# Attention output of five batches with tokens on rows, turned by the DMA crossbar, in a fused attention and expert kernel

## The chip, the cores and the metric

The kernel runs on one core of one Trainium2 chip. A core has a matrix engine (PE), a vector engine (DVE), a scalar engine (ACT), a general engine (POOL) that also issues the loads here, and a queue engine (SP) that issues DMAs. The metric is device time of one execution in microseconds. The kernel before was timed three times: 159.49, 161.36 and 158.82 us, median 159.49. Beside this stands one profiled execution with its trace.

## What is computed

Eight batches of 576 tokens. The first stage is an attention of 8 heads of 64 dimensions, in which keys and values are averaged over 8 tokens, so that each head has 72 pooled keys:

```python
k_p = k.reshape(B, H, Sp, pool, D).mean(axis=3)          # v_p likewise
scores = scale * np.matmul(q, k_p.transpose(0, 1, 3, 2))
attn = np.exp(scores - max); attn /= attn.sum(-1) + 1e-09
attn_out = np.matmul(attn, v_p)                          # [8, 8, 576, 64]
x = attn_out.transpose(0, 2, 1, 3).reshape(B, S, 512)
```

The second stage takes x. A gate `x @ w_gate` has four logits a token, of which the two largest are kept and made into weights. Each of four experts is a causal attention of one head of 64 dimensions over the 576 tokens, with its own projections; its output goes through `wo[e]`, is multiplied by the gate's weight of that token and added up into out [8, 576, 512] float32.

## The kernel before, in words

All orders are written out by hand: a long string `SEQ` (line 591) of tokens `name:batch@bank`, which a loop translates into instructions. PE, ACT, DVE and POOL each run their instructions in the order in which they come in this string; a `d` behind a token puts a copy on DVE instead of ACT. SP's queue runs its DMAs in the same order. PSUM has eight banks, and a token says which one its product fills.

The 576 tokens of a batch are cut into four tiles of 128 and a tail of 64; two batches make a pair, whose tails share one tile. For each batch the tokens are, in order of dependence:

- `L_k`, `L_q`, `L_v`: loads, issued by POOL (line 118), ten DMAs a batch, into three rotating buffers of each kind (`NRAW`). They turn float32 into bf16 on the way. POOL also runs the causal masks `a` (lines 471 and 479) between them.
- `PK`, `kc`, `kt`: PE pools the keys by a product with a small matrix, DVE turns them, a copy makes them bf16. `PV`, `vc`: the same for values. `u`: DVE turns q (line 255).
- `E`, `e`: scores of all heads, with the 96 padded pooled keys on partitions and tokens along columns; ACT takes the exponential into `eta` (line 292).
- `D`, `d`, `x`: PE adds the exponentials up by a product with ones (`onesd`), in which every sum stands on 32 partitions; ACT takes its logarithm (line 311) and the exponential of minus that (line 315), which is one over the sum, into `rza`.
- `O`, `o`: PE multiplies the pooled values with `eta`, 32 value dimensions of a head a strip; DVE multiplies the product with `rza` and writes bf16 into `xT` (lines 329 and 338), which has the 512 features on partitions and tokens along columns. This is the form that the second stage needs.
- `V`, `v`: expert values and gate logits of a tile of tokens. `g`: ten steps of the gate. `P`, `p`: queries and keys of experts, in pairs. `S`, `s`: expert scores and their exponential (line 462) into `etb`. `B`, `bz`, `bg`, `b`: product with the values and a column of ones, one over the sum, times the gate (lines 514, 516, 521), into `osc`, with tokens on rows.
- Then `osc` is turned into `oT`. For batches 0, 1, 6 and 7 by PE (`T`, line 198) and a copy (`t`); for batches 2 to 5 by the DMA crossbar (`F`, function `crossbar`, lines 546 and 549), issued on SP.
- `Y`, `y`: the product with `wo` and its copy to `ofin`, which SP writes out (lines 580 and 584).

For batch 0 the first stage works on halves of 256 tokens. Copies share line 180 and products share line 189, so they are told apart by their tiles.

Of the kernel before, what the change touches and what calls it, by code (L numbers as in the profile page):

```python
# [21 lines left out]
def kernel(  # L22
# [26 lines left out]
    PAIRW = 128 * NPC  # L49
# [41 lines left out]
    oscs = bufs(4, [128, NTC, 128], BF16, "osc")  # L91
    oTs = bufs(4, [128, PAIRW], BF16, "oT")
# [114 lines left out]
    def mcols(b):  # L207
        return slice(640 * (b % 2), 640 * (b % 2) + MAIN)

    def tcols(b):  # L210
        return slice(MAIN + 64 * (b % 2), MAIN + 64 * (b % 2) + TAIL)

# [31 lines left out]
    def vc(b, bank, dve):  # L244
        copy(dve, vps[b % 2][:], psum[0:KR, bank, :].rearrange("j (h d) -> j h d", d=D))
# [72 lines left out]
    def Ov(b, bank, g, t):  # L318
        got = pieces(b, g)
        for j, cols, o in got:  # L320
            for u in range(2) if g == 2 else [t]:
                for i, h, eta in heads(b, j, cols):
                    at_ = o * 2 + TAIL * u if g == 2 else o
                    mm(psum[32 * i : 32 * i + 32, bank, at_ : at_ + eta.shape[1]], vps[b % 2][:, h, u::2], eta)

    def ov(b, bank, dve, g, t):
        xT, rz = xt(b), part(rzas[b % 2], b, g)
        if g == 2:
            nc.vector.tensor_tensor(
                out=xT[:, :, tcols(b)].rearrange("p (g t) n -> p g t n", t=2),  # L330
# [4 lines left out]
        else:  # L335
            got = pieces(b, g)
            m = mcols(b).start
            nc.vector.tensor_tensor(  # L338
                out=xT[:, 2 * got[0][0] + t : 2 * got[-1][0] + t + 1 : 2, m + got[0][1].start : m + got[0][1].stop],
                in0=psum[:, bank, :].rearrange("p (g n) -> p g n", g=len(got)), in1=rz, op=MULT,  # L340
            )

    def V(b, bank, c):
        for fc in range(NFC):
            wide(psum[:, bank, 0:VG], xt(b)[:, fc, 128 * place(b, c) : 128 * place(b, c) + 128], wvg[:, fc, :],
# [65 lines left out]
    def pcols(b, nm, h):  # L411
        if nm == "t":
            return tcols(b), MAIN, TAIL
        m, c, n = mcols(b).start, (0 if h is None else HALF * h), (MAIN if h is None else HALF)
        return slice(m + c, m + c + n), c, n

    def P(b, bank, nm, ep, h=None):
        jobs = [(m, e) for m in "qk" for e in range(NEP)] if nm == "t" else [(nm, ep)]
        cols, _, n = pcols(b, nm, h)
        for j, (m, e) in enumerate(jobs):  # L420
            for fc in range(NFC):
                wide(psum[:, bank, n * j : n * j + n], wqk[m, e][:, fc, :], xt(b)[:, fc, cols],
                   start=(fc == 0), stop=(fc == NFC - 1))

    def p(b, bank, dve, nm, ep, h=None):
        qk = qks[b % 2]
        _, c, n = pcols(b, nm, h)
# [57 lines left out]
    def span(b, part):  # L485
        if 2 <= b < B - 2:
# [244 lines left out]
```

## Time and profile before

| | |
|---|---|
| median of three runs | 159.49 us (158.82 to 161.36) |
| the profiled execution, its own time | 159.26 us |
| its span, first to last instruction | 157.6 us |
| PE, ACT, DVE, POOL busy | 91%, 85%, 79%, 57% of the span |
| loads issued by POOL | 15.21 MB in 60240 packets |
| `oT<-osc` crossbar DMAs on SP | 16 |
| PE's mean granted clock | 0.969 |

In the profile, a line of a group of instructions has the source line, the engine, the operation, the tile written and those read, the shape, the count, then the busy time in us, the mean duration of one in ns, and the idle time of the engine just ahead of them with what ended it. Products on PE overlap, so that the busy time of a group is that of their union. The line of a queue has packets, MB, and the time of the packets as a share of the 16 DMA engines' time; it can exceed 100% since a DMA engine has more than one packet under way. "DMA to landing" is the time from the issue to the completion. A window shows busy us of PE, PEld (the weight loads), DVE, ACT and POOL, each with the number of instructions, then the granted clock, the DMA engines' share, and GB/s.

### The profile page before, as it was taken

What the parts mean: (1) busy time and instruction counts of PE and PEld (TensorE: products, weight loads), DVE (VectorE), ACT (ScalarE), POOL (GpSimd) and SP (SyncE); (2) the same over time, 40 slices, a digit from 0 to 9 for tenths busy, and PEclk for the clock granted to TensorE, in tenths of its full rate; (3) what the DMA queues carried; (4) which work ended last, traced back from release to release, by engine and by line L of the source; (5) the groups of instructions that cost most, each with busy time, mean ns of one, the idle gap of its engine ahead of it and who ended that gap; (6) DMA issues with size and microseconds to landing.
All of it is one profiled execution on the core that took longest, in us unless ns stands there. A gap on an engine that the chain in (4) does not pass through costs nothing.

```text
span 157.6 us, 5500 instructions
## 1 busy us (share of the span) xinstructions
PE 143.9 (91%) x2155; PEld 82.8 (53%) x2155; DVE 124.4 (79%) x412; ACT 133.7 (85%) x249; POOL 90.5 (57%) x162
## 2 busy tenths in 40 slices
PE   6876798988999999999999899999999999999940
PEld 2333565545456356446545564857576665557620
DVE  1513567697999989998999889999998998898840
ACT  3016778999899999999999899999999999899740
POOL 6997479976989799897986342004500343533000
PEclk9998579999999999999999999999999999999996
DMA  2999999999999999999999994512213064487994
GB/s 19 161 173 180 181 179 179 188 179 182 180 182 180 180 180 181 178 249 181 180 245 249 179 148 108 37 50 60 80 28 104 8 177 131 124 320 264 344 354 146
DMA packets 70635, 26.20 MB, mean 166 GB/s; under 512 B 65744, under 2 KB 66000, under 8 KB 70608
## 3 DMA queue, kind: packets, MB, share of 16 engines
q0 software_dynamic: 60240, 15.21, 99.7%
q1 hardware_dynamic: 10144, 10.23, 21.2%
q10 hardware_dynamic: 224, 0.39, 0.9%
q8 instruction: 17, 0.28, 0.7%
q14 instruction: 10, 0.08, 0.2%
HBM read 30.42 MB, written 9.44 MB: 253 GB/s over the span
## 4 chain that ended last, share of the span: by engine, by line
PE 53%; DMA 23%; POOL 14%; issue 3%; DVE 2%; POOLq 0%; DVEq 0%
PE psum L189 52%; DMA kraw<-in_k_dram 18%; DMA qraw<-in_q_dram 5%; POOL kraw L118 4%; POOL vraw L118 3%; POOL qraw L118 3%; POOL etb L479 2%; PE psum L198 1%; POOL wst_q L131 1%; POOL wst_k L131 1%; DVE qT L255 1%; POOL wop L131 0%; DVE osc L521 0%; DVE ofin L180 0%; DVE G L406 0%
## 5 line engine op out<-in xcount | busy, mean ns | idle before, releaser
L462 ACT ACTIVATE etb<-psum 128x1024 bf16<-128x1024 f32 x48 | 47.6, 1033 | 1.1 <-PE psum L189 1.0
L479 POOL TENSOR_SCALAR_AFFINE_SELECT etb<-etb 128x256 bf16<-128x256 bf16 x64 | 25.5, 412 | 37.9 <-ACT etb L462 36.7
L292 ACT ACTIVATE eta<-psum 96x1024 bf16<-96x1024 f32 (+1 forms) x48 | 36.1, 812 | 4.7 <-PE psum L189 4.2
L118 POOL DMA_DIRECT2D qraw<-in_q_dram x32 | 21.2, 669 | 4.8 <-DMA vraw<-in_v_dram 2.2
L189 PEld LDWEIGHTS <-etb 128*128 128x128 bf16 x480 | 18.7, 97 | 7.2 <-issue 2.8
L338 DVE TENSOR_TENSOR xT<-psum,rza 128x512 bf16<-128x512 f32 x32 | 20.8, 684 | 1.7 <-ACT rza L315 1.4
L118 POOL DMA_DIRECT2D vraw<-in_v_dram x24 | 18.6, 777 | 6.2 <-DMA kraw<-in_k_dram 3.6
L189 PE MATMUL psum<-vaug,etb 128*128 128x65 bf16 x480 | 20.6, 193 | 0.1
L189 PE MATMUL psum<-xT,wqp 128*128 128x64 bf16 (+2 forms) x136 | 20.2, 282 | 0.1
L189 PE MATMUL psum<-wvg,xT 128*128 128x260 bf16 x144 | 20.0, 274 | 0.1
L189 PE MATMUL psum<-wop,oT 128*128 128x512 bf16 (+1 forms) x74 | 19.8, 374 | 0.2 <-DVE oT L180 0.2
L189 PE MATMUL psum<-xT,wkp 128*128 128x64 bf16 (+2 forms) x136 | 19.8, 279 | 0.0
L118 POOL DMA_DIRECT2D kraw<-in_k_dram x24 | 18.6, 785 | 1.7 <-POOLq L715 0.8
L521 DVE TENSOR_TENSOR osc<-psum,gt 128x256 bf16<-128x256 f32 (+2 forms) x40 | 16.5, 421 | 1.0
L189 PEld LDWEIGHTS <-xT 128*128 128x128 bf16 x144 | 12.7, 97 | 7.2 <-issue 3.7
L189 PE MATMUL psum<-qk 64*128 64x64 bf16 (+4 forms) x192 | 15.6, 277 | 0.2 <-ACT etb L462 0.2
L189 PE MATMUL psum<-eta,vp 96*32 96x64 bf16 (+2 forms) x272 | 14.1, 301 | 1.1 <-DVE vp L180 0.8
L189 PE MATMUL psum<-qT,kpT 32*128 32x64 bf16 (+2 forms) x272 | 12.7, 281 | 2.6 <-DVE qT L255 2.3
L255 DVE STREAM_TRANSPOSE qT<-qraw 128x576 f32<-128x576 f32 (+2 forms) x18 | 11.9, 690 | 3.7 <-DMA qraw<-in_q_dram 3.5
L180 ACT COPY ofin<-psum 128x512 f32<-128x512 f32 (+1 forms) x22 | 12.6, 591 | 1.6 <-PE psum L189 1.5
L180 DVE CAST qk<-psum 128x512 bf16<-128x512 f32 (+1 forms) x22 | 13.3, 611 | 0.7 <-PE psum L189 0.6
L315 ACT ACTIVATE rza<-rza 128x512 f32<-128x512 f32 (+1 forms) x24 | 12.5, 529 | 0.3
(75 smaller groups left out, 216.5 us busy)
## 6 DMA issues: line engine op xcount, KB each, us to landing
out_dram<-ofin SPq DMA_DIRECT2D x31, 256.0 KB, 3.5
kraw<-in_k_dram POOLq DMA_DIRECT2D x24, 192.0 KB, 7.8
qraw<-in_q_dram POOLq DMA_DIRECT2D x32, 144.0 KB, 7.6
vraw<-in_v_dram POOLq DMA_DIRECT2D x24, 192.0 KB, 7.2
out_dram<-ofin SPq DMA_DIRECT2D x7, 128.0 KB, 2.6
wst_q<-in_moe_wq_dram POOLq DMA_DIRECT2D x1, 256.0 KB, 7.4
wst_k<-in_moe_wk_dram POOLq DMA_DIRECT2D x1, 256.0 KB, 8.0
wst_v<-in_moe_wv_dram POOLq DMA_DIRECT2D x1, 256.0 KB, 8.3
```

Of the source, the lines that this page charges most:

```text
L118: nc.gpsimd.dma_start(out=dst, in_=src)
L131: nc.gpsimd.dma_start(out=dst, in_=src)
L180: (nc.vector.tensor_copy if dve else nc.scalar.copy)(out=out, in_=in_)
L189: nc.tensor.matmul(out=out, lhsT=lhsT, rhs=rhs, start=start, stop=stop)
L198: nc.tensor.transpose(out=out[s], in_=in_[:, s], identity=ident[0:n, 0:n])
L255: nc.vector.transpose(out=dst.rearrange("p (a s n) -> p a n s", s=32, n=2), in_=src.rearrange("p (a n d) -> p a n d", n=2, d=32))
L292: nc.scalar.activation(out=dst, in_=src, func=EXP, scale=ATT_EXP_SCALE)
L315: nc.scalar.activation(out=rz, in_=rz, func=EXP, scale=-1.0)
L338: nc.vector.tensor_tensor(out=xT[:, 2 * got[0][0] + t : 2 * got[-1][0] + t + 1 : 2, m + got[0][1].start : m + got[0][1].stop], in0=psum[:, ...
L462: nc.scalar.activation(out=et[:, ep, :, eo : eo + n], in_=psum[:, bank : bank + 2, 0:n], func=EXP, scale=MOE_EXP_SCALE,)
L479: nc.gpsimd.affine_select(out=blk, in_=blk, pattern=[[0, 2], [1, 128]], compare_op=ISGE, fill=0.0, base=0, channel_multiplier=-1,)
L521: nc.vector.tensor_tensor(out=osc(b, ep)[:, own, :].rearrange("p c (e d) -> p e c d", e=2), in0=o[:, :, :, 0:HD], in1=gt.to_broadcast([128 ...
```

## The change

Batches 3 to 7 no longer use `D`, `d`, `x`, `O` and `o`. A column is added to the pooled values of each head, with ones scaled as the values are. `N` (five a batch) multiplies, for each of the 8 heads, 128 tokens of `eta` as the stationary operand with the 65 columns of that head; the result has tokens on rows, and the last column of a head is its sum. `nz` inverts the 8 sums of a tile on DVE, and `n` multiplies the 8 x 64 outputs with them into `xn` in bf16, tokens on rows. `G` (three a batch: two of 128 x 1024, one of 64 x 512) has the DMA crossbar turn `xn` into `xT`, issued on SP. `rza`, which batches 0 to 2 still use, lies in the memory of `xn`.

`xT` is laid out tile by tile (`[128, NPC, NFC, 128]`), in another order of the features, which `rows_of` gives to those who read it; `vc` writes the values in a permuted order to match. The ones of the batch's tail need a pad behind `eta`. At the other end, `oT` and `osc` are laid out anew, and the crossbar turns the outputs of batches 0 to 5 (`F`, `turn_y`, three a batch: two of 128 x 512, one of 64 x 256), and PE those of batches 6 and 7. For batches 0 and 1 the product `B` is cut into two parts an expert pair instead of three. The string `SEQ` is another one throughout: order, banks, and which engine makes which copy; it has six more warm-up products.

```diff
-    vps = bufs(2, [KR, H, D], BF16, "vp")
+    vps = bufs(2, [KR, H, D + 1], BF16, "vp")
-    etas = bufs(2, [KR, H, S], BF16, "eta")
-    rzas = bufs(2, [128, 2, S], FP32, "rza")
-    xTs = bufs(2, [128, NFC, PAIRW], BF16, "xT")
+    etaws = bufs(2, [KR, H * S + TAIL], BF16, "eta")
+    etas = [t[:, 0 : H * S].rearrange("k (h s) -> k h s", h=H) for t in etaws]
+    xns = bufs(2, [128, NTC, DM], BF16, "xn")
+    rzas = [t[:].rearrange("p c n -> p (c n)").bitcast(FP32)[:, 0 : 2 * S].rearrange("p (g s) -> p g s", g=2) for t in xns]
+    rzns = bufs(2, [128, H], FP32, "rzn")
+    xTs = bufs(2, [128, NPC, NFC, 128], BF16, "xT")
...
+        for t in vps:
+            nc.vector.memset(t[:, :, D : D + 1], 0.0)
+            for c in range(3):
+                nc.vector.memset(t[32 * c : 32 * c + 24, :, D : D + 1], DSC)
+        for t in etaws:
+            nc.vector.memset(t[:, H * S :], 0.0)
...
+    def rows_of(fc):
+        return 2 * (fc % 2) + fc // 2
...
+    def Nx(b, bank, c):
+        c0 = 128 * c if c < 4 else MAIN - 64 * (b % 2)
+        for h in range(H):
+            mm(nat(bank)[:, h, 0 : D + 1], etaws[b % 2][:, S * h + c0 : S * h + c0 + 128], vps[b % 2][:, h, :])
+
+    def nx(b, bank, step, c):
+        rows = slice(0, 128) if c < 4 else half(b)
+        o, rz = nat(bank)[rows], rzns[c % 2][rows]
+        if step == "nz":
+            nc.vector.reciprocal(out=rz, in_=o[:, :, D])
+        else:
+            nc.vector.tensor_tensor(
+                out=xns[b % 2][rows, c].rearrange("p (t h r) -> p h t r", t=2, h=H),
+                in0=o[:, :, 0:D].rearrange("p h (t r) -> p h t r", t=2),
+                in1=rz.unsqueeze(2).unsqueeze(3).to_broadcast([rz.shape[0], H, 2, 32]), op=MULT,
+            )
+
+    def turn_x(b, k):
+        xn, o = xns[b % 2], b % 2
+        if k == 2:
+            nc.sync.dma_start(out=xt(b)[:, 4, :, half(b)], in_=xn[half(b), 4, :], transpose=True)
+        else:
+            m = mains(b).start + 2 * k
+            nc.sync.dma_start(out=xt(b)[:, m : m + 2].rearrange("p c f n -> p (c f) n"),
+                              in_=xn[:, 2 * k : 2 * k + 2].rearrange("p c n -> p (c n)"), transpose=True)
...
-    def crossbar(b, ep, tail):
...
+    def turn_y(b, k):
+        own, oT = oscs[b % 2], oTs[b // 2 % 2]
+        if k == 2:
+            nc.sync.dma_start(out=oT[:, 4, :, half(b)], in_=own[half(b), 4:6].rearrange("p e n -> p (e n)"), transpose=True)
+        else:
+            nc.sync.dma_start(out=oT[:, mains(b), k, :], in_=own[:, 6 * k : 6 * k + 4].rearrange("p c n -> p (c n)"), transpose=True)
...
     SEQ = """
...
+        E1:3@24 L_v1:4 bz01:0 B10:0@6 bg01:0 b01:0 e10:3 L_v2:4 B00:1@0 bz10:0 F2:0 O20:2@7 bg10:0 PK:4@1 b10:0 e11:3
...
+        F1:0 kt:4 nz0:3 n0:3 N1:3@2 S10:1@6 p_q0:2 nz1:3 P_k1:2@1 n1:3 s10:1 u0:4 G0:3 N2:3@2 P_t0:2@0 p_k1:2 a10:1
...
+        nz3:3 n3:3 E1:4@46 p_k0:2 L_q0:5 PV:4@0 G1:3 e11:4 S10:2@2 L_q1:5 vc:4d B11:1@1 s10:2 L_q2:5 V0:3@6 bz11:1
+        V3:2@0 bg11:1 L_q3:5 e10:4 v0:3d N4:3@2 b11:1 a10:2 Y3:0@7 nz4:3 L_v0:5 Y1:0@6 v3:2 n4:3 y3:0 N0:4@4 N1:4@0
+        L_v1:5 y1:0 G2:3 P_k1:3@2 nz0:4 nz1:4 g0:2 n1:4 L_v2:5 V1:3@3 n0:4 p_k1:3 S12:2@0 v1:3 S11:2@6 g1:2 PK:5@2
...
+        a02:3 V2:4@2 N3:5@0 p_q1:4d G0:5 Y2:0@4 v2:4 a01:2 nz3:5 S11:3@6 a01:3 n3:5 y2:0 PK:6@5 s11:3 g6:3 S00:3@2 kc:6
+        S10:3@0 P_q0:4@4 s00:3 kt:6d a11:3 u0:6 L_k0:7 P_k0:4@5 s10:3 p_q0:4d L_k1:7 E0:6@26 p_k0:4 g7:3 u1:6 N2:5@0
+        L_k2:7 e00:6 B01:2@4 nz2:5 n2:5 a10:3 P_t0:4@5 e01:6 a00:3 N4:5@2 bz01:2 g8:3 L_q0:7 G1:5 Y0:1@0 g9:3 bg01:2
...
+        PK:7@3 b10:3 vc:6 S12:4@0 kc:7 S11:4@6 F1:2 S10:4@4 s12:4 P_k0:5@2 kt:7d g4:4 s11:4 g5:4 a12:4 N1:6@0 P_q0:5@3
```

More of the change, by code (lines that the diff above doesn't have):

```diff
@@ L244, in vc @@
     def vc(b, bank, dve):
-        copy(dve, vps[b % 2][:], psum[0:KR, bank, :].rearrange("j (h d) -> j h d", d=D))
+        copy(dve, vps[b % 2][:, :, 0:D].rearrange("j h (t r) -> j h t r", t=2),
+             psum[0:KR, bank, :].rearrange("j (h r t) -> j h t r", r=32, t=2))
     def half_bank(bank):
@@ L521, in bv @@
             nc.vector.tensor_tensor(
-                out=osc(b, ep)[:, own, :].rearrange("p c (e d) -> p e c d", e=2),
+                out=oscs[b % 2][:, osc(b, ep, part), :].rearrange("p c (e d) -> p e c d", e=2),
                 in0=o[:, :, :, 0:HD],
@@ L526, in bv, with T, t @@
             )
[L528 to L549 removed]
+    def T(b, bank, ep, part):
+        at_ = osc(b, ep, part).start
+        for i in range(len(span(b, ep, part))):
+            flip(half_bank(bank)[:, 128 * i : 128 * i + 128], oscs[b % 2][:, at_ + i, :])
+    def t(b, bank, dve, ep, part):
+        places = span(b, ep, part)
+        cols = half(b) if places == [4] else slice(0, 128)
+        src = half_bank(bank)[:, 0 : 128 * len(places)].rearrange("p (c n) -> p c n", n=128)
+        copy(dve, oTs[b // 2 % 2][:, run(places), ep, cols], src[:, :, cols])
+    def turn_y(b, k):
+        own, oT = oscs[b % 2], oTs[b // 2 % 2]
+        if k == 2:
+            nc.sync.dma_start(out=oT[:, 4, :, half(b)], in_=own[half(b), 4:6].rearrange("p e n -> p (e n)"), transpose=True)
+        else:
+            nc.sync.dma_start(out=oT[:, mains(b), k, :], in_=own[:, 6 * k : 6 * k + 4].rearrange("p c n -> p (c n)"), transpose=True)
     def Y(b, bank, c):
[L552 removed]
         last = (b, c) == (B - 1, 4)
```

225 lines of the change are left out of this document (101 added, 124 removed).

## The prediction

> **What bounds the kernel now.** I read the page first: the shares of the engines, the slices of the DMA engines, and the chain that ended last.
>
> ```profile
> span 157.6 us, 5500 instructions
> ...
> PE 143.9 (91%) x2155; PEld 82.8 (53%) x2155; DVE 124.4 (79%) x412; ACT 133.7 (85%) x249; POOL 90.5 (57%) x162
> ...
> DMA  2999999999999999999999994512213064487994
> ...
> q0 software_dynamic: 60240, 15.21, 99.7%
> ...
> PE 53%; DMA 23%; POOL 14%; issue 3%; DVE 2%; POOLq 0%; DVEq 0%
> ```
>
> Two things share this span. Up to slice 24, some 95 us, the DMA engines are full; what fills them is q0, the loads of q, k and v. In the chain a quarter is DMA and the rest mostly PE. The chain in order of time says where one gives way to the other:
>
> ```profile
> 78.11 11.13 DMA kraw<-in_k_dram
> 89.24 0.04 issue
> 89.28 53.32 PE psum L189 x785
> ```
>
> The last k load, that of batch 7, is issued at 78.11 and lands at 89.24. PE's pooling of it (token `PK:7`) runs at that moment, and from there PE alone carries the chain. So I split the span at 89.2 and look at the engines on both sides:
>
> ```profile
> 0.00:89.20 89.20, 81.77 (x1241) 44.07 (x1242) 68.31 (x217) 74.35 (x140) 74.09 (x121) 0.96 1.70 181
> ...
> 89.20:150.80 61.60, 61.45 (x910) 38.44 (x909) 55.41 (x193) 58.61 (x109) 16.40 (x42) 1.00 0.61 138
> 150.80:157.60 6.80, 0.70 (x4) 0.31 (x4) 0.71 (x4) 0.76 (x2) 0.00 (x0) 0.77 0.68 228
> ```
>
> Columns are PE, PEld, DVE, ACT, POOL, then clock, DMA share and GB/s. Before 89.2 the loads' share is 1.70: they cannot come sooner. After it PE is busy without a break, ACT for 95% (58.61 of 61.60), DVE for 90%; the last 6.8 us are the last tiles' way out. The time is therefore the landing of k of batch 7 (89.24), plus what is left to do after it (68.4), plus what lies outside the span, 159.26 - 157.6 = 1.66. The change moves both of the first two terms.
>
> **What the change takes from the engines.** Rows of the groups, whole run:
>
> ```profile
> L311 ACT ACTIVATE rza<-psum 128x512 f32<-128x512 f32 (+1 forms) x24 | 11.4, 494 | 1.0 <-PE psum L189 0.9
> L315 ACT ACTIVATE rza<-rza 128x512 f32<-128x512 f32 (+1 forms) x24 | 12.5, 529 | 0.3
> L338 DVE TENSOR_TENSOR xT<-psum,rza 128x512 bf16<-128x512 f32 x32 | 20.8, 684 | 1.7 <-ACT rza L315 1.4
> L329 DVE TENSOR_TENSOR xT<-psum,rza 128x256 bf16<-128x256 f32 x8 | 3.4, 420 | 0.7 <-PE psum L189 0.4
> L514 DVE RECIPROCAL rzb<-psum 128x4 f32<-128x4 f32 (+2 forms) x40 | 7.0, 176 | 1.3 <-PE psum L189 0.7
> L180 DVE COPY oT<-psum 128x256 bf16<-128x256 bf16 (+1 forms) x17 | 3.9, 255 | 0.5 <-PE psum L198 0.2
> L198 PE MATMUL psum<-ident,osc 128*128 128x128 bf16 x40 | 5.2, 220 | 0.0
> L189 PE MATMUL psum<-eta,vp 96*32 96x64 bf16 (+2 forms) x272 | 14.1, 301 | 1.1 <-DVE vp L180 0.8 <-ACT rza L311 0.2
> L189 PE MATMUL psum<-eta,onesd 96*32 96x64 bf16 (+2 forms) x136 | 9.5, 302 | 0.0
> L189 PE MATMUL psum<-vaug,etb 128*128 128x65 bf16 x480 | 20.6, 193 | 0.1
> L189 PE MATMUL psum<-wvg,xT 128*128 128x260 bf16 x144 | 20.0, 274 | 0.1
> ```
>
> ACT: `d` and `x` (the logarithm and the exponential of the sums) go for five batches, 15 of 24 in each row: 15/24 x (11.4 + 12.5) = 14.9 us less.
> DVE: `o` goes, 20/32 x 20.8 + 5/8 x 3.4 = 15.1 us less. In its place stand 25 `nz` and 25 `n`. No row shows them; `n` writes 512 bf16 a partition from PSUM as L338 does, so it lies between 420 (half of it) and 684 ns, and I take 684; `nz` inverts 8 columns, and I take L514's 176. 25 x 0.86 = 21.5 us more (14.9 at the low end). Of the copies of the turned output (`t`) for batches 0 and 1 nine go on DVE, 9/17 x 3.9 = 2.1 (and three on ACT, 0.8 at the same price), and four triples `bz`, `bg`, `b` with their fixed parts, 12 x 0.176 = 2.1. Net 2.2 us more.
> Together ACT and DVE lose 13.5 us, 6.7 each if the new split of copies between them evens it out.
> PE: `D` and `O` of five batches go. By instructions, 160 of 272 and 80 of 136, that is 8.3 + 5.6 us of busy time; 200 products of 65 columns come, at 20.6/480 = 43 ns 8.6 us; half of the turns go, 2.6. Net 7.9 us less, by busy times that overlap.
> The new memsets stand ahead of the first landing, beside DMA; without that cover the ten of them would cost some 1.8 us at L514's price. The permuted `vp` copy and the other order inside `xT` I set at nothing: same sizes, read by the same instructions, and the copies stand beside PE's work; a quarter more on eight copies of L338's 684 ns would be 1.4.
>
> **What is left after batch 7's k.** The new order puts `PK:7` later: counted from the two orders, ACT has after it
>
> ```profile
> L462 ACT ACTIVATE etb<-psum 128x1024 bf16<-128x1024 f32 x27 | 26.6, 1031 | 0.7 <-PE psum L189 0.5
> L180 ACT COPY ofin<-psum 128x512 f32<-128x512 f32 (+1 forms) x18 | 10.4, 588 | 1.6 <-PE psum L189 1.5
> L292 ACT ACTIVATE eta<-psum 96x1024 bf16<-96x1024 f32 (+1 forms) x12 | 9.0, 812 | 0.5 <-PE psum L189 0.2
> L315 ACT ACTIVATE rza<-rza 128x512 f32<-128x512 f32 (+1 forms) x8 | 4.1, 515 | 0.1
> L311 ACT ACTIVATE rza<-psum 128x512 f32<-128x512 f32 (+1 forms) x8 | 3.7, 474 | 0.0
> L180 ACT CAST vaug<-psum 128x256 bf16<-128x256 f32 x5 | 1.9, 381 | 0.0
> ```
>
> 24 large `s` in place of 27 (-3.0), 6 `e` in place of 12 (-4.5), no `x` and `d` (-7.8), four more `y` (+2.3), five more `v` (+1.9, and their small second copies, at most as much again), the rest about even: -10 to -11. 58.6 - 10.8 = 47.8, which at the same 95% takes 50.3 us. PE's 61.45 loses five of its 17 `V` (20 products of 144, 2.8), all of `O` and `D` (92 and 40 by the old order, 4.8 + 2.8), 46 of the 65-column products (2.0), three `E` and small things, and gets 80 `N` (3.4): near 51 too. With the last 6.8 us I put 58 after the landing (56 to 60) where there were 68.4. So the change wins 10.4 us here, **if k of batch 7 lands no later.**
>
> **What it does to the landing of k.** Eight `F` and nine `G` now stand ahead of `PK:7`; before, the first `F` came after it. Thirteen are issued by SP ahead of the last k load: `F` of batches 0 and 1, `G` of 3 and 4, `G0:5`. Do they slow the loads? Queues in three windows (packets, MB, share of 16 engines, which is 32 us of engine time in a window of 2): 60 to 62, loads alone; 68 to 70, with output writes; 109.1 to 110, one `F` of 128 x 512 and no loads (14.4 us of engine time):
>
> ```profile
> q0 software_dynamic: 1436, 0.36, 182.1%
> ```
> ```profile
> q0 software_dynamic: 571, 0.14, 72.1%
> q1 hardware_dynamic: 221, 0.42, 60.3%
> ```
> ```profile
> q1 hardware_dynamic: 538, 0.13, 71.5%
> ```
>
> Alone, loads run 1436 packets in 2 us, 22.3 ns each on 16 engines. With SP's queue beside them they fall to 571: what SP sends takes the loads' turns. A write packet costs 0.603 x 32 us / 221 = 87 ns, so a write of 128 packets 0.7 us. The `F` moved 0.13 MB in 256-byte packets, 512 and some semaphore writes, at 0.715 x 14.4 us / 538 = 19.1 ns. Sizes go with the shapes: `F` has 512 + 512 + 128 packets a batch, `G` 1024 + 1024 + 256. The thirteen: 2 x 1152 + 2 x 2304 + 1024 = 7936. At 19.1 ns on 16 engines 9.5 us, at the loads' 22.3 11.1; I take **9.5**. One write fewer is issued ahead (five, not six): **-0.7**.
>
> [...]
>
> There is more. Before's first pair of `F` fell among the last loads, 92 to 94 and 94 to 96:
>
> ```profile
> q0 software_dynamic: 810, 0.20, 252.3%
> q1 hardware_dynamic: 60, 0.01, 7.2%
> q8 instruction: 1, 0.02, 3.0%
> ```
> ```profile
> q1 hardware_dynamic: 555, 0.13, 46.8%
> ```
>
> With 60 crossbar packets beside them the loads moved 810, not 1436, while their share rose to 252%: packets were held. In the same window one instruction transfer took 3% of 32 us, about 1 us, on one engine; I read it as the crossbar waiting for that engine and the others for the crossbar. Lost: 1436 - 870 = 566 packets, 0.8 us for the pair, 0.4 us for each `F` or `G`. That is one sample; the next 2 us are short too, partly since loads ran out, and with them it is 0.75 each. Lower end nothing. I take 0.4 x 13 = **5.2**. k of batch 7 then lands 9.5 - 0.7 + 5.2 = 14.0 us later, at 103.2, and PE stands before `PK:7` meanwhile.
>
> The waits on the crossbar itself: landing of the pair at 89 us, then of all 16:
>
> ```profile
> DMA to landing us min/median/max: 6.8/7.1/7.5
> ```
> ```profile
> DMA to landing us min/median/max: 2.2/2.4/7.5
> ```
>
> `P_k1:3` waits for `G1:3`; between them ACT has two large `e`, one `s`, one `v`, two `y`, about 4.9 us by their rows. A landing of 7 or more stops PE there some 2 to 3 us, with `V1:3`, `S` and all later products behind it, and on SP's queue the writes of `y` and `G2:3` behind the earlier `G`. It happens while loads are late anyway, so I add nothing; without that cover, 2 to 3 us for each of two or three such places. After the loads a `G` should land in 2.4 to 3.5 us, within the order's distances.
>
> **Forecast**: 89.24 + 14.0 + 58 + 1.66 = 162.9, about 163 us (160.5 to 167 with the spread of the last terms).
>
> **The rivals.**
> 1. The plan holds (faster). Crossbar packets ride in turns that loads leave, at half a turn (9.6 ns, two packets being in flight in each engine by the 182%), 4.7 us: 89.24 + 4.7 - 0.7 + 58 + 1.66 = 152.9. The engines' own sum agrees: 157.6 - 6.7 + 1.66 = 152.6. For it: `PK:7` stands later in the order, with three large `s` and six `e` more ahead of it and seven `d` and six `x` fewer, some 4 us of ACT's work by the rows, so a delay of that size costs nothing. Against: 571 beside 221.
> 2. Displacement alone, nothing held: 89.24 + 8.8 + 58 + 1.66 = 157.7, within 2%.
> 3. Each crossbar holds the loads as the whole pair did, at the 27 ns that 555 packets took among loads (0.468 x 32 us / 555): 13.4 - 0.7 + 9.8 = 22.5, and 171.4 us.
>
> The delay decides at 10.4 us: above it the change loses.
>
> **How the numbers follow.** Forecast 0.45, rival 1 0.20, rival 2 0.20, rival 3 0.15. About 2% (3.2 us) is what a measurement of this kernel tells from no change. Faster: rival 1, 0.20. Same (156.3 to 162.7): rival 2 and a good fifth of the forecast's case, 0.30. Slower: 0.50. The range leaves out half of rival 1 and half of rival 3: 153 to 169.
>
> **What would show it.** `PK:7` at or after 100 us, released by the DMA of kraw, with ACT and PE idle ahead of it; loads at fewer than 1400 packets in 2 us wherever `F` or `G` are under way; packets of q0 over 200% there; 56 to 60 us from that landing to the end; ACT near 126 and DVE near 119 us busy. I am wrong if k of batch 7 lands before 98 us, or if what follows it takes 65.

## The result, and the profile after

The changed kernel takes 178.68 us (median of four, 175.44 to 180.59) beside 160.06 for the kernel before (median of four, 158.82 to 161.36). The ratio is 1.106, with a 95% interval of 1.083 to 1.129: slower, by some 17 us where 3.5 were forecast. The ratios in this part leave out executions that were disturbed (of the changed kernel's four, 180.59 and 179.55 us), so they can lie under the quotient of two medians, and differences that are given as "by the ratios" are worked out on 159.5 us.

The profiled execution of the changed kernel is its longest, 180.59 us, with a span of 178.9. From its page, the span, the shares of the engines, the slices of the DMA engines, the queue that carries crossbar and writes, and the chain by engine and by line (the chain's last line ends cut, as the page has it):

```profile
span 178.9 us, 5417 instructions
...
PE 151.4 (85%) x2088; PEld 85.7 (48%) x2101; DVE 122.4 (68%) x405; ACT 129.9 (73%) x237; POOL 90.2 (50%) x162
...
DMA  4999999999999999996999849999965376458876
...
q1 hardware_dynamic: 24512, 13.77, 35.9%
...
PE 45%; DMA 23%; ACT 10%; DVE 8%; POOL 6%; issue 4%; ACTq 1%; DVEq 0%; POOLq 0%
```

Before, the DMA engines were full up to some 95 us (slice 24 of the line in the prediction) and at 0 to 6 tenths from there to some 138. Now they are full up to slice 29, some 130 us, with dips in slices 19 and 23 to 24 (80 to 85 and 98 to 107 us), which the kernel before did not have. ACT and DVE are less busy in all, as the change meant, and everything takes longer.

The chain in order of time (start, length, what):

```profile
66.66 10.20 DMA xT<-xn
76.91 6.28 PE psum L197 x69
...
85.77 9.59 DMA xT<-xn
95.40 8.33 PE psum L197 x68
104.24 1.04 ACT etb L501
105.74 1.42 POOL kraw L120 x2
107.21 0.77 POOL kraw L120
107.98 0.78 POOL etb L518 x2
108.76 1.90 POOL qraw L120 x3
110.66 12.18 DMA qraw<-in_q_dram
```

Where the chain of before had loads, this one has crossbar DMAs of 10.20 and 9.59 us. They are `G` of batches 3 and 4. Behind them comes PE, then ACT, then POOL, and only then the next loads. Read from the top: a product waits for its turned x, ACT waits for a product, a mask on POOL waits for ACT, and the loads of batch 7 stand behind that mask on POOL's queue.

POOL's own timeline shows the same link for batch 6. In brackets is the idle time ahead, and what ended it:

```profile
69.81 1.53 POOL L120 DMA_DIRECT2D vraw<-in_v_dram  x2
81.34 1.32 POOL L518 TENSOR_SCALAR_AFFINE_SELECT etb<-etb 128x256 bf16<-128x256 bf16 x3 [10.00 <-ACT etb L501]
82.61 2.29 POOL L120 DMA_DIRECT2D kraw<-in_k_dram  x3
```

POOL stood for 10.00 us in front of a mask, with the loads of batch 6 behind it; this is what empties slice 19. The k loads of batch 7 were issued at 105.69 to 107.21 us (76.59 to 78.11 before), and the last landed at 114.65 (89.24 before). From there to the end of the span it took 64.3 us (68.4 before).

How PE stood, by its waits (total, times, longest), and the landing of the nine `G` issued between 55 and 115 us (shortest, median, longest):

```profile
PE psum L197 <- DMA xT<-xn: 9.9, 4, 4.6
```
```profile
DMA to landing us min/median/max: 3.1/8.3/10.2
```

And the windows of PE, PEld, DVE, ACT and POOL, then the granted clock, around the first of these stops and the second:

```profile
66.00:72.00 6.00, 4.41 (x63) 2.66 (x64) 3.27 (x9) 4.49 (x8) 4.49 (x7) 1.00 1.67 181
72.00:77.00 5.00, 0.36 (x10) 0.24 (x7) 2.29 (x10) 0.55 (x2) 0.00 (x0) 0.71 1.66 185
77.00:83.00 6.00, 6.00 (x72) 2.99 (x72) 1.62 (x5) 3.36 (x6) 1.52 (x4) 0.68 1.18 171
...
95.00:101.00 6.00, 5.60 (x44) 2.94 (x44) 2.05 (x6) 2.46 (x5) 1.18 (x3) 0.50 1.57 160
```

From 72 to 77 us PE is busy for 0.36 us, ACT for 0.55, POOL not at all. The stop of PE costs twice: the granted clock, 1.00 at 66 to 72 us, is 0.68 in the 6 us behind the stop, and 0.50 at 95 to 101, behind the second stop. (In `early_loads` below, it is 0.62 at 72 to 78 us and 0.63 at 96 to 102, each behind such a stop.)

### The profile page after: what moved, and what is told of

The parts are those of the page before. It is cut to its first block, busy times and chain, and to the rows that moved or that the text cites. A ratio compares the mean times of both kernels' runs of the same rounds, so it can differ in the third digit from the quotient of the medians.

```text
span 178.9 us, 5417 instructions
## 1 busy us (share of the span) xinstructions
PE 151.4 (85%) x2088; PEld 85.7 (48%) x2101; DVE 122.4 (68%) x405; ACT 129.9 (73%) x237; POOL 90.2 (50%) x162
## 4 chain that ended last, share of the span: by engine, by line
PE 45%; DMA 23%; ACT 10%; DVE 8%; POOL 6%; issue 4%; ACTq 1%; DVEq 0%; POOLq 0%
PE psum L197 43%; DMA xT<-xn 13%; DMA qraw<-in_q_dram 10%; ACT eta L300 4%; POOL kraw L120 3%; ACT etb L501 2%; POOL qraw L120 2%; DVE xT L346 2%; PE psum L185 1%; ACT ofin L188 1%; ACT qk L188 1%; DVE qT L263 1%; ACTq L624 1%; DVE osc L567 1%; PE psum L206 1%
## 5 line engine op out<-in xcount | busy, mean ns | idle before, releaser
L197 PE MATMUL psum<-xT,wkp 128*128 128x64 bf16 (+2 forms) x136 | 22.9, 308 | 5.3 <-DMA xT<-xn 5.3
L197 PE MATMUL psum<-wvg,xT 128*128 128x260 bf16 x144 | 21.4, 283 | 6.3 <-DMA xT<-xn 4.6
L197 PE MATMUL psum<-xT,wqp 128*128 128x512 bf16 (+2 forms) x136 | 21.1, 290 | 0.1
L188 ACT CAST qk<-psum 128x512 bf16<-128x512 f32 (+1 forms) x22 | 11.0, 511 | 10.5 <-PE psum L197 10.2
L188 ACT COPY ofin<-psum 128x512 f32<-128x512 f32 (+1 forms) x28 | 15.6, 588 | 4.1 <-PE psum L197 4.1
L197 PE MATMUL psum<-wop,oT 128*128 128x512 bf16 (+1 forms) x62 | 17.8, 376 | 0.5 <-DVE oT L188 0.3
L197 PE MATMUL psum<-qk 64*128 64x64 bf16 (+4 forms) x192 | 17.4, 294 | 0.5 <-ACT etb L501 0.3
L367 DVE TENSOR_TENSOR xn<-psum,rzn 128x512 bf16<-128x512 f32 (+1 forms) x25 | 17.1, 689 | 0.8
L197 PE MATMUL psum<-qT,kpT 32*128 32x64 bf16 (+2 forms) x272 | 13.6, 294 | 3.4 <-DVE qT L263 2.4
L197 PEld LDWEIGHTS <-wkp 128*128 128x128 bf16 x136 | 9.4, 105 | 11.9 <-DMA xT<-xn 5.9
L263 DVE STREAM_TRANSPOSE qT<-qraw 128x576 f32<-128x576 f32 (+2 forms) x18 | 11.9, 689 | 4.2 <-DMA qraw<-in_q_dram 4.2
```

Of the source, the lines that this page charges most:

```text
L188: (nc.vector.tensor_copy if dve else nc.scalar.copy)(out=out, in_=in_)
L197: nc.tensor.matmul(out=out, lhsT=lhsT, rhs=rhs, start=start, stop=stop)
L263: nc.vector.transpose(out=dst.rearrange("p (a s n) -> p a n s", s=32, n=2), in_=src.rearrange("p (a n d) -> p a n d", n=2, d=32))
L367: nc.vector.tensor_tensor(out=xns[b % 2][rows, c].rearrange("p (t h r) -> p h t r", t=2, h=H), in0=o[:, :, 0:D].rearrange("p h (t r) -> p ...
```

## The experiments

The theory from the two traces: `G` costs in two ways, by the DMA time that it takes from the loads, as forecast, and by the waits of PE for its landing, which had been set at nothing. Rivals: traffic alone, the early `F`, the new order as such, the layouts.

The runs in one table; each is explained below. The last column is the landing of the last k load of batch 7, in the one execution of each that was profiled. The ratios are to executions of the kernel before that were timed beside the run (medians 159.23 to 160.06 us).

| run | median us | ratio to before | k of batch 7 |
|---|---|---|---|
| kernel before | 160.06 | | 89.24 |
| changed kernel | 178.68 | 1.106 (1.083 to 1.129) | 114.65 |
| g_nowait | 170.00 | 1.065 (1.061 to 1.070) | 102.71 |
| no_g | 160.45 | 1.011 (1.003 to 1.019) | 95.08 |
| no_early_f (two executions) | 179.65 | | 116.63 |
| before_more | 176.40 | 1.109 (1.102 to 1.116) | 105.33 |
| early_loads | 174.95 | 1.096 (1.091 to 1.101) | 99.77 |
| early_nowait | 170.09 | 1.055 (1.050 to 1.060) | 107.28 |
| g_plain | 175.35 | 1.091 (1.084 to 1.099) | 110.40 |
| g_quarter | 169.21 | 1.047 (1.038 to 1.055) | 102.83 |
| old_order | 159.10 | 0.996 (0.993 to 0.998) | 89.86 |
| late_only | 164.66 | 1.025 (1.020 to 1.031) | 89.33 |
| late_spread | 162.44 | 1.018 (1.014 to 1.021) | 90.29 |
| late_nowait | 161.36 | 1.012 (1.006 to 1.019) | 89.54 |

**Waits or traffic.** In `g_nowait` the readers of x in batches 3 to 7 read a tile that never changes:

```diff
-            wide(psum[:, bank, 0:VG], xt(b)[:, place(b, c), rows_of(fc), :], wvg[:, fc, :],
+            wide(psum[:, bank, 0:VG], xt(b)[:, place(b, c), rows_of(fc), :] if b < 3 else wqk["q", 0][:, rows_of(fc), :], wvg[:, fc, :],
```

The products of `P` are changed in the same way.

> The changed kernel, in which the products V and P of batches 3 to 7 read a constant tile and not xT; every G is issued as before and moves the same bytes, but nobody waits for its landing. (The output is that of other data.) Two theories. Waits: the products of a batch stop PE until its G has landed, ACT stops behind PE, the masks on POOL behind ACT, and the loads behind the masks; then with no wait left k of batch 7 lands at 99 to 104 us (not 114.65) and the time is 160 to 165 us. Traffic: it is the crossbar packets themselves that displace and hold the loads; then k of batch 7 still lands after 110 us and the time stays at 172 us or more.

In `no_g` the three DMAs of `G` in each batch are left out, in `no_early_f` those of `F` for batches 0 to 2 (two hunks of two kernels; each also fills the tile that nobody writes then, by memsets at the start):

```diff
     def turn_x(b, k):
-        xn, o = xns[b % 2], b % 2
...
+        pass
...
     def turn_y(b, k):
+        if b < 3:
+            return
```

> The changed kernel without G: xn is written, nothing turns it, V and P read what xT holds. (The second stage of batches 3 to 7 works on old data.) Both theories expect 152 to 157 us; against the run in which G moves its bytes and nobody waits, the difference is what G's traffic costs: by the waits theory at most 8 us, by the traffic theory 15 or more.

> The changed kernel without F for batches 0 to 2, so that their outputs are not turned (the output rows of these batches are left wrong). This takes 2304 of the 7936 packets ahead of the last k load, and 6 of 13 crossbar DMAs. Traffic: 14 us shrink by a third, 170 to 174 us. Waits: G lands sooner only where an F was ahead of it on the queue; 172 to 177 us.

`before_more` is the kernel before with ten crossbar DMAs that nobody waits for, spread over batches 1 to 4:

```diff
+    def more(b, k):
+        src = etas[b % 2][:].rearrange("k h s -> k (h s)")[:, 1024 * k : 1024 * k + 1024]
+        dst = wst["qkv"[turned[0] % 3]][:].rearrange("p e g t d -> p (e g t d)")[:, 0 : 8 * KR]
+        nc.sync.dma_start(out=dst.rearrange("p (c n) -> p c n", n=KR), in_=src, transpose=True)
...
```

> The kernel before, with ten more crossbar DMAs on SP (one behind the exponentials of batch 1, three each behind those of batches 2, 3 and 4), each of 96 x 1024 from eta into a dead tile that nobody reads: 768 packets each, 7680 in all, and no wait. Traffic, by the terms of the prediction: 7680 x 19.1 ns / 16 = 9.2 us and 10 x 0.4 us, k of batch 7 lands about 13 us later (102) and the time is 170 to 173 us. Displacement alone: 167 to 169. If the packets ride in turns that the loads leave: 159 to 162.

`no_g` has the ratio 1.011, `g_nowait` 1.065, the changed kernel 1.106. So, by the ratios, the traffic of `G` costs 5.5 in 100 (8.7 us) with nobody waiting, the waits another 4.1 (6.5 us), and the new order without any `G` 1.1 (1.7 us). The expectation for `g_nowait` was missed from above (160 to 165 said), but its landing of k, 102.71, is the one that the theory of the waits named; the theory of traffic alone asked for more than 110. The DMA engines show the waits too. In the changed kernel next to nothing was under way at 82.6 to 84.1 us, 100.6 to 104.0 and 106.0 to 107.2, together 6.1 of the 11.9 us by which its k lands later than that of `g_nowait`; in `g_nowait` there is no such gap before the landing. PE is not free of stops there: between 60 and 115 us it waits 6.2 us for turned q, whose loads came late, the longest time 3.8 us. That is part of what the traffic costs.

`no_early_f` took 177.49 and 181.81 us, which is no gain over the changed kernel; both of its expectations (170 to 174 and 172 to 177) were missed from above. So, as far as two executions show, the early `F` cost nothing beside the waits. `no_g` was expected at 152 to 157 and took 160.45: the new order, without its crossbar DMAs of x, is 1% over the kernel before and no gain.

`before_more` shows the traffic without any other change; 170 to 173 us were expected and 176.40 measured. The queues in the same ten us, 52 to 62, in the kernel before and in `before_more` (packets, MB, share of 16 engines):

```profile
q0 software_dynamic: 7122, 1.78, 181.2%
```
```profile
q0 software_dynamic: 4145, 1.04, 108.7%
q1 hardware_dynamic: 2129, 0.53, 50.7%
```

2129 packets of the crossbar's queue stand where 2977 packets of loads are missing, 1.4 for each. Up to 59 us it is 1.1 (1412 in place of 1541); most of the rest falls in one stop from 59.2 to 60.1 us, in which hardly a packet of either queue starts. With its 7680 packets k of batch 7 lands 16.1 us later; the prediction's prices (19.1 ns on 16 engines, 0.4 us for each DMA) give 13.2.

**Is it that loads are issued late?** In `early_loads` the loads of batches 4 to 7 stand up to 50 tokens earlier in the string, so that they are ahead of masks that wait. The core of the edit, for the k loads of batch 7:

```diff
-        S10:3@0 P_q0:4@4 s00:3 kt:6d a11:3 u0:6 L_k0:7 P_k0:4@5 s10:3 p_q0:4d L_k1:7 E0:6@26 p_k0:4 g7:3 u1:6 N2:5@0
-        L_k2:7 e00:6 B01:2@4 nz2:5 n2:5 a10:3 P_t0:4@5 e01:6 a00:3 N4:5@2 bz01:2 g8:3 L_q0:7 G1:5 Y0:1@0 g9:3 bg01:2
...
+        s00:2 g1:3 a03:2 V3:4@3 g2:3 S01:3@0 s03:3 g3:3 g4:3 v3:4 S02:2@4 g5:3 bz01:1 N0:5@6 L_k0:7 s01:3 bg01:1
+        P_k1:4@3 b01:1 L_k1:7 nz0:5 a00:2 F2:1 n0:5 s02:2 L_k2:7 B10:2@2 p_k1:4d S02:3@0 S01:2@6 F0:1 a02:2 bz10:2
```

> The changed kernel whole, with one edit: in the order, the loads of batches 4 to 7 stand up to 50 tokens earlier on POOL's queue, ahead of masks that wait for ACT, though never ahead of the last reader of their buffer. Nothing is left out. In the changed kernel k of batch 7 landed at 114.65 us, and in the run in which nothing waited for G at 102.7; DMA carried no loads around 82 to 84 and 102 to 107 us. Theory (a product waits for a crossbar, ACT waits for the product, a mask on POOL waits for ACT, and the loads stand behind the mask): the gaps close, k of batch 7 lands at 103 to 108 us, the time is 167 to 172. Rival (the stopped PE is what costs, whatever the loads do): k of batch 7 lands earlier too, but PE comes to its pooling after 111 us with the data long there, and the time stays at 175 or more. Second rival (the loads were late through the traffic alone): the landing stays at 112 or more.

> Both edits together: the loads of batches 4 to 7 up to 50 tokens earlier on POOL's queue, and the products that read xT in batches 3 to 7 read a constant tile, so that nobody waits for G, which moves its bytes as before (what is computed from x in these batches is left wrong). With waits and early loads 174.95 us were measured, without waits and with the old place of the loads 170.0, without any G 160.45. Theory (the two losses are separate: stopped PE at the waits, late loads through the traffic; each has its own cure): k of batch 7 lands at 95 to 100 us, PE is at its pooling by 97 to 100, the time is 161 to 165. Rival (the traffic takes the loads' turns wherever they stand, and earlier issue gains nothing where DMA is full): k of batch 7 lands at 101 or later and the time is 167 to 171.

With the waits in place, k of batch 7 now lands at 99.77 us, 15 earlier, and it helps little: 174.95 us. PE comes to it at 114.00 with the data long there, and it still waits as long for crossbar DMAs. From the timeline of PE in `early_loads`, and from PE's waits there:

```profile
114.00 0.29 PE L197 MATMUL psum<-kraw,poolk 96*32 96x128 bf16 x2
```
```profile
PE psum L197 <- DMA xT<-xn: 9.9, 5, 4.7
```

My theory of the late loads fell here (it said 167 to 172 us); the rival, that the stopped PE is what costs, fits. The late loads are a consequence of the stop, and curing them alone gains 1 in 100, which the intervals do not tell from nothing. `early_nowait` says the same from the other side, as its second expectation had it (k at 101 or later, 167 to 171 us): its landing is later (107.28, in the longest of its four executions) than without the early loads, and the ratio falls only from 1.065 to 1.055. That the loads share full DMA engines with `G` wherever they stand (in `early_nowait` the engines are at 9 tenths in every slice from the second to the 28th, up to 119 us) is the likely reason; no run takes it apart. The four ratios form a square: with waits 1.106 and 1.096, without 1.065 and 1.055. Waits are worth 4 in 100 in either column, early loads 1 at most.

**The crossbar, or any DMA?** In `g_plain` the same bytes go as ordinary copies in 256-byte pieces:

```diff
...
-            nc.sync.dma_start(out=xt(b)[:, m : m + 2].rearrange("p c f n -> p (c f) n"),
-                              in_=xn[:, 2 * k : 2 * k + 2].rearrange("p c n -> p (c n)"), transpose=True)
+            for r in range(2):
+                nc.sync.dma_start(out=xt(b)[:, m + r],
+                                  in_=xn[:, 2 * k : 2 * k + 2].rearrange("p c (f n) -> p (c f) n", n=128)[:, r::2])
```

> The changed kernel in which G copies without turning: the same bytes by the same queue, in 256-byte pieces, as ordinary DMAs (two in the place of each crossbar DMA). What is computed from it is left wrong, since xn is not turned; all instructions of the engines and all waits stand. If the crossbar itself holds the loads and lands late because of that, G lands in under 5 us among loads in place of 7 to 10, k of batch 7 lands at 103 to 108, the time is 163 to 171. If any traffic of this size in pieces of 256 bytes does the same, G still lands in 7 us and more, k of batch 7 lands at 111 or later and the time is within 2% of the changed kernel, 175 to 182.

In `g_quarter` each `G` turns a quarter of its columns, and everyone waits as before:

```diff
...
-            nc.sync.dma_start(out=xt(b)[:, m : m + 2].rearrange("p c f n -> p (c f) n"),
-                              in_=xn[:, 2 * k : 2 * k + 2].rearrange("p c n -> p (c n)"), transpose=True)
+            nc.sync.dma_start(out=xt(b)[:, m : m + 2].rearrange("p c f n -> p (c f) n")[:, 3:5],
+                              in_=xn[:, 2 * k : 2 * k + 2].rearrange("p c n -> p (c n)")[:, 384:640], transpose=True)
```

> The changed kernel in which each G turns only a quarter of its columns (128 x 256 in place of 128 x 1024, and 64 x 128 in place of 64 x 512), into pieces of xT that all of its readers touch: every product still waits for its G, the crossbar moves a quarter of the packets; the rest of xT is left as it was, so what is computed from it is wrong. Measured so far: whole G with waits 178.7, whole G without waits 170.0, no G 160.45 us. If what costs is the volume (G lands late because its own 1024 packets take turns with the loads): a small G lands in 3 to 5 us, k of batch 7 lands at 96 to 99, the time is 161 to 165. If what costs is standing behind loads that are already queued, whatever the size: a small G too lands in 6 us or more, PE waits as long at each place, and the time is 167 to 173.

Landing of `G` issued between 55 and 115 us, first in `g_plain`, then in `g_quarter`, and PE's waits for it in `g_quarter`:

```profile
DMA to landing us min/median/max: 2.3/7.2/9.1
```
```profile
DMA to landing us min/median/max: 2.3/6.2/7.8
```
```profile
PE psum L198 <- DMA xT<-xn: 4.5, 3, 2.2
```

An ordinary copy of half the pieces of a `G` lands in 7.2 us in the median, a crossbar DMA in 8.3, a quarter of a crossbar DMA in 6.2. The two copies that stand for one `G` are complete 8.2 us after the first is issued, in the median of nine. So it is not the crossbar that makes the landing late, as the second expectation of `g_plain` had it (7 us and more, 175 to 182): what lands late is a DMA that is issued while loads fill the engines. Nor is it mainly its own size, since a quarter of the packets saves a quarter of the time; with no loads beside it a whole `G` landed in 2.3 to 4.8 us (`late_only`). `g_quarter` fell between its two expectations, in PE's waits (4.5 us in place of 9.9) and in time (166.9 us by the ratio; 161 to 165 and 167 to 173 were named). Beside `no_g` it costs 5.7 us by the ratios; a quarter of the 8.7 for whole traffic would be 2.2, and the rest is likely the wait. Copied or turned, the whole kernel takes about the same, 175.35 and 178.68 us with intervals that overlap; both land late beside loads, and that was the point.

**What is the other form worth where no loads run?** `old_order` has the layouts of the changed kernel (values, `xT`, `osc`, `oT`, `F`) and the order and the operations of before. In the string of before, the four `F` of each of batches 2 to 5 become the three of the new shape; beside that, one line of the changed functions differs:

```diff
-        if b < B - 2:
+        if 2 <= b < B - 2:
             got = [[0, 1, 2], [3, 4]] if b % 2 == 0 else [[5, 6, 7], [8, 4]] if ep == 0 else [[4, 5, 6], [7, 8]]
```

> The kernel before with the layouts of the changed one and nothing of G: the order of before, D, d, x, O and o for all batches, xT tile by tile, values permuted, two osc and two oT buffers, F in its new shape (128 x 512) for batches 2 to 5. Nothing is left out. The prediction set the permuted copies at nothing, with 1.4 us as the other end. If that holds: 158 to 160.5 us, k of batch 7 landing at 88.5 to 91. If the layouts cost, through slower o or through waits for an oT or osc buffer: 162 or more.

`late_only` is the same with `N`, `nz`, `n` and `G` for batches 6 and 7 alone; `late_spread` puts scores `S` between the `N`; `late_nowait` takes the waits from it, by the edit of `g_nowait` for batches 6 and 7. The first of the changed lines, of the order of before to `late_only`, and from there to `late_spread`:

```diff
-        e11:6 bz01:3 V0:4@3 bg01:3 b01:3 B11:3@0 v0:4 v1:5d E2:6@46 O11:6@1 g1:4 e21:6 D1:6@2 bz11:3 O01:6@3 e20:6
+        e11:6 bz01:3 V0:4@3 bg01:3 b01:3 B11:3@0 v0:4 v1:5d E2:6@46 N0:6@2 g1:4 e21:6 nz0:6 n0:6 N1:6@6 bz11:3 e20:6
```
```diff
-        e11:6 bz01:3 V0:4@3 bg01:3 b01:3 B11:3@0 v0:4 v1:5d E2:6@46 N0:6@2 g1:4 e21:6 nz0:6 n0:6 N1:6@6 bz11:3 e20:6
+        e11:6 bz01:3 V0:4@3 bg01:3 b01:3 B11:3@0 v0:4 v1:5d E2:6@46 N0:6@2 g1:4 e21:6 nz0:6 n0:6 S02:4@6 bz11:3 e20:6
```

> As the run with the order of before and the new layouts, but batches 6 and 7 alone use N, nz, n and G in place of D, d, x, O and o; these stand behind the last loads, so that no crossbar of x runs beside a load. Nothing is left out. Theory (the change is sound where no loads run: G lands in 2.4 to 3.5 us, ACT loses 15 us x 6/15 = 6.0, DVE gains 8.6 - 6.1 = 2.5, and ACT is what the stretch after k of batch 7 has least of): k of batch 7 lands at 88.5 to 91 as before, the stretch after it shrinks by 2 to 5 us, 154 to 158 us. Rival (a product that waits for a crossbar stops PE here too): 160 to 164, with PE idle 1 to 3 us at each G.

> Batches 6 and 7 alone use N, nz, n and G, as in the run late_only, but the order around them is spread: between two N stand scores S of batches 4 and 5, so that ACT has work while DVE runs n, and V and P stand further behind G; four copies go from DVE to ACT. Nothing is left out. In late_only PE and ACT stood in two places, with ACT busy 5.59 of 10 us at 100 to 110 and 5.14 at 120 to 130. Theory (only the distances were wrong there): both dips go, ACT is busy 9 of 10 us in each window, 154 to 158 us. Rival (PE or DVE is the limit by now, and what ACT is spared is worth nothing): no dips, but 159 to 162.

> The run late_spread (162.44 us: N, nz, n and G in batches 6 and 7 alone, order spread), with the products that read xT in batches 6 and 7 reading a constant tile, so that nobody waits for G; G moves its bytes as before; what is computed from x in these two batches is left wrong. It shows what the other form of the attention output is worth to the engines by itself, behind the loads. If the prediction's sum of the engines holds (ACT spared 6.0 us, DVE 2.5 more, PE some 3 less, ACT the limit): 154 to 157.5. If the products of 65 columns cost PE what the others did and PE is the limit: 159 to 162, and the remaining loss against the kernel before is not the wait for G.

The layouts cost nothing: `old_order` is 0.4% under the kernel before, too little to call it faster.

`late_only` was expected at 154 to 158 and took 164.66, near the second expectation (160 to 164). Its windows (PE, PEld, DVE, ACT, POOL) show two dips of ACT; its chain has four `n` on DVE (0.68 to 0.69 us each) in the first, and a `G` in the second:

```profile
100.00:110.00 10.00, 8.90 (x157) 5.67 (x156) 9.03 (x32) 5.59 (x12) 1.18 (x3) 1.00 0.38 68
...
120.00:130.00 10.00, 7.64 (x106) 4.59 (x104) 7.96 (x23) 5.14 (x10) 1.40 (x4) 1.00 0.61 116
```
```profile
122.46 4.76 DMA xT<-xn
```

By the ratios, spreading the order brings 1.2 us, and taking the waits away another 0.8, which is within the intervals. Then 161.36 us are left, 2.3 over `old_order` by the medians and 2.7 by the ratios. The same windows of `late_nowait`:

```profile
100.00:110.00 10.00, 9.49 (x161) 5.83 (x161) 8.89 (x33) 7.54 (x14) 1.64 (x5) 1.00 0.54 62
110.00:120.00 10.00, 9.62 (x147) 6.39 (x146) 8.48 (x37) 8.83 (x17) 2.37 (x6) 1.00 0.32 90
120.00:130.00 10.00, 9.56 (x119) 6.03 (x120) 8.51 (x27) 7.81 (x13) 2.40 (x6) 1.00 0.59 107
```

PE stays at 9.5 to 9.6 of 10, ACT falls to 7.5 to 8.8: PE is the fullest engine here. It is not quite full, though: in the same windows of `old_order` PE has 9.95 of 10, and what takes the other 0.4 us is not shown. The second expectations hold for `late_nowait` (159 to 162), and nearly for `late_spread`. Even with no load, no wait and the order spread, the other form gains nothing on these two batches. Page lines of `old_order` and of `late_nowait`:

```profile
PE 143.5 (91%) x2140; PEld 83.2 (53%) x2155; DVE 124.6 (79%) x422; ACT 133.7 (84%) x249; POOL 90.8 (57%) x162
```
```profile
PE 143.9 (90%) x2121; PEld 83.8 (53%) x2139; DVE 125.4 (79%) x429; ACT 130.7 (82%) x240; POOL 90.8 (57%) x162
```

ACT is spared 3.0 us (four copies of about half a microsecond were given to it; 4.8 in `late_only`, without these), of 6 expected. PE, which was to be spared 3, has as much as before. Why its total does not fall is open; by rows, `D` and `O` give up 7.2 us in `late_spread` and `N` takes 4.3. With `N` in five batches it falls by 3.6 us (140.3 in `no_g`, 143.9 before), where 7.9 were forecast. `N` loads 128 columns of weights for each product of 65 (in the changed kernel 200 loads of 96x128, 101 ns each), but no run here takes that apart from the rest.

## Why the prediction was right or wrong

The direction was right and the size wrong: 163 was said, with a range up to 169, and 178.68 came (176.5 by the ratio). By the ratios, the waits are 6.5 of these 13.5 us; most of the rest is the stretch behind k of batch 7, which took 63.5 to 65.7 us where 58 was put. The traffic came out as priced.

- **The step that failed first: "It happens while loads are late anyway, so I add nothing".** The place was named rightly (`P_k1:3` behind `G1:3`, PE stopped), its landing too ("7 or more"; median 8.3), and it was priced at nothing. Measured, waits are worth 6.5 us by the ratios (1.106 beside 1.065 in `g_nowait`). The cover was not there: the stopped PE stops ACT and POOL's masks (10.00 us of POOL), the loads stand behind the masks, and so the DMA engines, the very thing that was to hide the wait, ran empty for 6 us, and k of batch 7 landed at 114.65 us where 103.2 was put. The stop itself cannot be made up either, as `early_loads` shows. The other end that the prediction gave, "2 to 3 us for each of two or three such places", 4 to 9 us, would have held it.
- **The traffic, "9.5" and "5.2", was right in size.** k of batch 7 was put at 103.2 us; without waits it landed at 102.71. In `no_g`, where only `F` stand ahead of it, 95.08. So `G` ahead of it cost 7.6 us (its seven were priced at 9.5), and `F` with the new order 5.8 (4.5). In `before_more` the same prices give 13.2 us, and 16.1 were measured. The 19.1 ns a packet (204 GB/s: 0.13 MB in 0.64 us of full engines) are one sample: with the engines to themselves, crossbar DMAs moved 462 packets from 63.5 to 63.9 us in `g_nowait`, 285 GB/s and 13.9 ns each on 16 engines, and 454 from 64.35 to 64.75 us in the changed kernel, 289 GB/s and 14.1 ns.
- **"I put 58 after the landing (56 to 60)" was too little.** It took 64.3 us in the changed kernel, 65.7 in `g_nowait`, 63.5 in `no_g`. The windows of `no_g`, split at 97.2 us, where PE starts on that k:

```profile
0.00:97.20 97.20, 87.31 (x1344) 48.84 (x1349) 76.66 (x242) 79.19 (x142) 76.04 (x126) 1.00 1.73 168
97.20:150.00 52.80, 50.49 (x723) 31.88 (x731) 45.03 (x155) 47.80 (x90) 14.39 (x36) 1.00 0.72 165
150.00:158.60 8.60, 2.45 (x23) 1.28 (x22) 2.06 (x11) 2.22 (x7) 0.00 (x0) 0.78 0.57 205
```

47.80 us of ACT behind that start, as forecast, but at 91% of 52.8, not at 95%; the way out of the last tiles took 8.6 us, not 6.8; and PE came to k 2.1 us after it had landed, since it still had work ahead. 2.5 + 1.8 + 2.1 = 6.4 us lie between the 57.1 that the prediction's own terms give (50.3 + 6.8) and these 63.5. PE's share came out as put ("near 51"; 50.49). And of the "10.4 us" won there, half is work that the new order has moved ahead of that k: ACT has 79.19 us there, where before it had 74.35.
- **"Together ACT and DVE lose 13.5 us, 6.7 each" holds for the rows and not for the engines.** The sums of all groups fell by 8.7 us on ACT (148.7 to 140.0) and by 4.7 on DVE (140.3 to 135.6), 13.4 together. The engines' own totals on the page fell by 3.8 (133.7 to 129.9) and 2.0 (124.4 to 122.4). A row counts each instruction to its end, while the next one has begun: before, ACT's rows exceed its total by 15.0 us over 249 instructions, DVE's by 15.9 over 412. After, where both have more gaps, it is 10.1 us over 237 and 13.2 over 405. So part of what the rows win is no time of the engine.
- **Prices of new operations.** `n` was put at 684 ns and took 689; `nz` at 176, took 199; a product of 65 columns at 43 ns, took 54 (10.9 us for 200, the row below; 4.3 us for 80 in `late_nowait`, 54 again, and 10.4 for 200 in `no_g`, 52).

```profile
L197 PE MATMUL psum<-vp,eta 96*128 96x65 bf16 x200 | 10.9, 199 | 0.1
```

- **The signs.** PE's start on k at or after 100 us: yes, 114.92, though with no idle time of PE ahead of it, since PE came straight from other products. ACT near 126 and DVE near 119: no, 129.9 and 122.4. What follows the landing was to take 56 to 60, and 65 was named as proof of the contrary: 64.3. Loads at fewer than 1400 packets in 2 us where crossbar DMAs run: yes. Their share over 200% there: no. The row of the loads' queue in the changed kernel, 85 to 95 us, and the two queues in 1.3 us of these ten, 91.3 to 92.6:

```profile
q0 software_dynamic: 4388, 1.10, 127.1%
```
```profile
q1 hardware_dynamic: 44, 0.01, 34.2%
q0 software_dynamic: 11, 0.00, 12.5%
```

In the mean of the ten us, 878 packets in 2 us at 127%, nothing seems held. But packets were held, in short stops like the second one shown: 11 packets of loads in 1.3 us, while those under way took up to 1.4 us each. `g_nowait` has five such stops before k of batch 7 lands, of 0.5 to 1.4 us, together 4.3 us where the prediction put 5.2; `no_g` has two, the kernel before has none up to its landing. Each of the five begins 0.8 to 1.4 us after the start of an instruction transfer (queue q8) that falls beside crossbar DMAs, as in the sample on which the 0.4 us rested. Not every such transfer brings a stop, and no run tests the reason that the prediction read into it, that the crossbar waits for the transfer's engine. So the term is borne out in size and in kind; the named sign, a share over 200%, was the wrong one.
- **The rivals.** The plan that holds (152.9) failed on the engines' sum as well: without any `G`, `no_g` takes 160.45. Displacement alone (157.7) puts the landing at 98.0, and without waits it was 102.71. The heavier holding (171.4) came nearest in time, but by luck: it puts the landing at 111.7 by traffic alone, and traffic alone gave 102.71. None of the three priced the wait.

## What to carry to other kernels

Before a DMA is put between two engines, price its landing at the place where it will stand, beside the traffic of that moment: a median of 2.4 us for the crossbar DMAs of the kernel before, most of them behind the loads, became medians of 6.2 to 8.3 beside loads, for a quarter as for the whole, turned or copied. Here a wait of PE was to be hidden by loads that themselves hung on PE (POOL stood for 10.00 us of it); follow the chain once round (product, exponential, mask, load, product) before setting it at nothing. And where PE, ACT and DVE were busy for 100, 95 and 90% of a stretch, before, behind k of batch 7, taking work from one of them won nothing (ACT spared 3.0 us in `late_nowait`, 161.36 us beside 159.10 of `old_order`); compare the engines' totals, not sums of rows.

## What the runs showed of the hardware that was not expected

- The DMAs issued on SP beside loads landed late, and a quarter of the size saved only a quarter of the time: 8.3 us in the median for whole `G`, 6.2 for a quarter, 7.2 for plain copies of half the size, each over the nine or more that were issued between 55 and 115 us.
- Behind a stop of PE of 4.6 us the granted clock was 0.68 for the following 6 us, and behind a second one, of 4.4 us, 0.50; the whole execution had 0.917.
- Beside crossbar DMAs, and not once in the kernel before up to its landing, nearly all packets of all queues stood still for 0.5 to 1.4 us at a time: five times in `g_nowait` before its landing, 4.3 us together, each just behind an instruction transfer. In the changed kernel 55 packets moved in the 1.3 us from 91.3, where 16 engines had moved 715 in the 1.3 us before.
- Neighbouring instructions overlapped: before, the durations of ACT's 249 instructions add up to 156.0 us and its busy time is 133.7, 90 ns for each; DVE's 412 to 143.2 and 124.4, 46 ns. So the rows of these two engines add up to more than their busy time.
